# A long convolution's working store kept in runs of four channels instead of runs of two

## The chip, the cores and the metric

The kernel runs on one core of one Trainium2 chip. The metric is the device time of one execution in microseconds (us). The core has a matrix engine (TensorE, PE in the profile, with its weight loads on a row of their own, PEld), a vector engine (DVE), a scalar engine (ACT), a general engine (POOL), and a queue that issues transfers between the chip's memory and the on-chip store (SP). The on-chip store, SBUF, has 128 partitions. TensorE writes its results into PSUM, which has eight banks of 512 floats in each partition. Everything is float32.

TensorE multiplies a *stationary* operand, which is loaded beforehand column by column, by a *moving* operand, which is streamed through. Both are read from SBUF through an access pattern: in each partition, which elements follow one another and with what steps. The change is about these patterns.

## What is computed

```python
def _attn_ref(x, v, pos_emb, w1, w2):              # x, v: (4, 12480, 128); pos_emb: (12480, 64)
    h_mlp = np.maximum(pos_emb @ w1, 0.0) @ w2
    h_filt = h_mlp * np.exp(-0.01 * np.arange(S))[:, None]
    u = x * v
    Uf = np.fft.rfft(u, n=2 * S, axis=1); Hf = np.fft.rfft(h_filt, n=2 * S, axis=0)
    y = np.fft.irfft(Uf * Hf[None], n=2 * S, axis=1)[:, :S, :]
    return x * y

def _moe_ref(x, w_in, w_out):                      # x: (49920, 128); w_in: (128, 2048)
    h = x @ w_in
    return (h * np.cos(h)) @ w_out
```

So: a gated long convolution of each of 128 channels over 12,480 positions, for four batches, and then a feed-forward block over all 49,920 rows.

## The kernel before

**The convolution** is a transform over the product N1 x N2 = 96 x 120, done as four matrix steps per batch, with products by a filter spectrum between the second and the third. All four work in place in one large SBUF tile, `slots`, of 64 channel pairs (`CB`) by 240 places by 2 channels. In the text a step is called by its function:

- `u`: the gated input x*v is folded and written into `slots` by `u_sums` (L406, POOL and DVE), two places with all 64 pairs at a time, from the loaded rows `xt`.
- `f1` (`f1_mm`, L414; evicted by `f1_evict`, L428): for each of 64 channel pairs and each channel i of the pair, the stationary operand is `u[:, b, 0:KE, i]`, which steps over places; the constant table `c1` (192 columns) moves. The result goes back into the same pair's part of `slots`, then called `parts`.
- `f2` (`f2_mm`, L450; `f2_product`, L464): for each of 96 frequencies k the table `w` is stationary and `parts[0:KE, :, k]`, all 64 pairs and both halves r, 256 columns, moves. The result is multiplied by the filter spectrum `h` and written, as `y`, into the places that k has left. The spectrum is computed once, beside the first batch (`f2_both_units`), kept in chip memory (`hd`) and loaded again for the other batches (`f2_units`). Two frequencies, k1 and k1+1, are handled as one unit j.
- `i1` (`i1_mm`, L485; `i1_evict`, L491): for each pair, `slots[0:N2, b, r*N1:..., i]` is stationary and the table `cs` (120 columns) moves; ACT copies one half out of PSUM and DVE writes sum and difference back into `slots`.
- `i2` (`i2_mm`, L510; `i2_out`): for each of 120 output positions in 30 groups of four, two products are accumulated: a made table `t` is stationary and `slots[0:N1, :, place, :]`, 128 columns, moves. The result is multiplied by x and stored.

So `parts` in `f2` and `slots` in `i2` move, and `slots` in `f1` and `i1` is stationary. With the tile laid out as pair, place, channel, a moving read over all channels at one place takes two neighbouring floats (8 bytes), then jumps 1,920 bytes to the next pair. A stationary read over places of one channel steps by two floats.

**The feed-forward block** is a long sequence of 1,568 steps: `moe_up` (a 512-column product into `ph`), three passes of ACT and DVE for the cosine gate, sums on POOL (`moe_sums`) and `moe_down` (products of 128 columns into the banks `acca` and `accb`; seven of them in each pair of steps).

**The order of the work** is written out by hand; every engine takes its instructions in that order. Before about 338 us there is the filter network, the filter's `f1`, the first batch's `f1`, `f2` and `i1`. From then on the steps of the feed-forward block and those of the convolution alternate: after each step `convolve()` (L989) advances the convolution until it has caught up with its share of steps (`F1_STEPS`, `F2_STEPS` and so on, L564). The helper `units` (L535) runs the units of one convolution step: it issues the matmuls of unit j in two parts and, between them, the eviction of unit j-1. From this point on `tiled[0]` is true, and `mm` (L129) issues every matmul as two, one for each half of the output's columns, which work in the array side by side; a float32 matmul is two records in the profile. So a product with 256 moving columns is four records.

Of the kernel before, what the change touches and what calls it, by code (L numbers as in the profile page):

```python
# [9 lines left out]
F32 = mybir.dt.float32  # L10
# [23 lines left out]
def kernel(  # L34
# [63 lines left out]
    CB = D // 2  # L98
    assert R * N2 == S and S + TAPS - 1 <= 2 * M and math.exp(DECAY * TAPS) < 2.0 ** -150
# [13 lines left out]
    hd = dram.tile([N1 // 2, N2, 2, CB, 4], F32, name="hd")  # L113
# [147 lines left out]
    def inverse_tables(pool):  # L261

        t = Tables(pool, nc.gpsimd, 4)
        part = t.whole([P, 1], [[1, 1]], channel_multiplier=1, name="part")
        part4 = t.whole([P, 1], [[1, 1]], base=1, channel_multiplier=4, name="part4")
        step = t.whole([P, P], [[1, P]], name="step")
        mid = t.whole([P, P], [[1, P]], base=-MID, name="mid")
        cs, (rows, tw_t) = third_table(pool), last_tables(pool)
        yield from t.sines(step, part, N2, [(cs[:, 0, 0:H + 1], 1), (cs[:, 1, 0:H + 1], 0)],
                           eighths=slice(0, H + 1, H))  # L270
        yield from t.sines(step[:, 1:H], part, N2,
                           [(cs[:, 0, H + 1:], 0), (cs[:, 1, H + 1:], 1)])
        yield from t.sines(step, part4, 4 * N1,
                           [(rows[:, i, :], q) for i, q in enumerate((0, 1, 2, 3))])
        yield from t.sines(mid, part4, TURN, [(tw_t[:, 0, :], 1), (tw_t[:, 1, :], 0)],
                           eighths=slice(H - 1, N2, H))
        t.finish(len(t.waiting))
        for kept, made in ((csd, cs), (rowsd, rows), (twd, tw_t)):
            nc.sync.dma_start(kept[:, :, :], made[:, :, :])
# [82 lines left out]
    def filter_out(pool, bank, aT, slots, j, w2_sb):  # L362

        ps = bank()
        for i, jj in enumerate((j, H - 1 - j)):
            nc.tensor.matmul(ps[0:FR, i * 2 * D:(i + 1) * 2 * D], aT[:, jj, 0:FR],
                             w2_sb[:, :], start=True, stop=True)
        above = pool.tile([FR, 2, CB, 2], F32, name="above", bufs=2)
        pj = ps[0:FR, :].rearrange("p (n b i) -> p n b i", n=4, i=2)
        nc.scalar.copy(out=above[:, :, :, :], in_=pj[:, 2:4])  # L370
        a = H - 2 - 2 * j
        for place, op in ((a, ALU.add), (ODD + a, ALU.subtract)):
            nc.vector.tensor_tensor(
                slots[0:FR, :, place:place + 2, :].transpose([0, 2, 1, 3]),
                pj[:, 1::-1], above[:, :, :, :], op=op)
# [14 lines left out]
    def clear_gap(u):  # L390

        nc.gpsimd.memset(u[:, :, H:ODD, :], 0.0)
# [13 lines left out]
    def u_sums(u, tiles, a, takers):  # L406
        both = tiles[0][:, :, :].rearrange("p h (n b i) -> p h n b i", n=UA, i=2)
        below, above = both[:, 0, ::-1, :, :], both[:, 1, :, :, :]
        for place, op, e in ((a, ALU.add, takers[0]), (ODD + a, ALU.subtract, takers[1])):
            e.tensor_tensor(u[0:R, :, place:place + UA, :].transpose([0, 2, 1, 3]),  # L410
                            below, above, op=op)


    def f1_mm(ps, u, b, i):  # L414

        mm(ps[0:KE, i * 2 * N1:(i + 1) * 2 * N1], u[:, b, 0:KE, i],
           c1[0:u.shape[0], :, :].rearrange("p r k -> p (r k)"))
# [10 lines left out]
    def f1_evict(ps, b, share):  # L428
        copy, negated = f1_takers(b, share)
        pj = ps[:, 0:4 * N1].rearrange("p (i r k) -> p r k i", i=2, r=2)  # L430
        copy(out=parts[0:ODD, :, :, b, :], in_=pj[0:ODD])
        yield
        copy(out=parts[ODD:KE, 0, :, b, :], in_=pj[ODD:KE, 1])
        negated(parts[ODD:KE, 1, :, b, :], pj[ODD:KE, 0])
        yield

    def f1_evict_filter(ps, b, share):

        copy, negated = f1_takers(b, share)
        pj = ps[:, 0:4 * N1].rearrange("p (i k) -> p k i", i=2)  # L440
        near, far = ftile[:, b, :, :], above[:, b, :, :]
        copy(out=near[0:ODD], in_=pj[0:ODD, 0:N1 + KF])
        copy(out=far[0:ODD], in_=pj[0:ODD, N1 + KF:])
        yield
        copy(out=near[ODD:KE, 0:N1], in_=pj[ODD:KE, N1:])
        negated(near[ODD:KE, N1:], pj[ODD:KE, 0:KF])
        negated(far[ODD:KE], pj[ODD:KE, KF:N1])
        yield

    def f2_mm(ps, w, k1, i, filt=False):  # L450


        k = k1 + i
        pi = ps[0:N2, :].rearrange("p (r b g i) -> p g r b i", r=2, g=2, i=2)[:, i]
        if not filt:
            mm(pi, w[:, i, :], parts[0:KE, :, k])
        elif k < KF:
            both = ftile[0:KE, :, k:k + N1 + 1:N1, :].rearrange("p b r i -> p r b i")
            nc.tensor.matmul(pi, w[:, i, :], both, start=True, stop=True)
        else:  # L460
            for r, src in enumerate((ftile[0:KE, :, k, :], above[0:KE, :, k - KF, :])):
                nc.tensor.matmul(pi[:, r], w[:, i, :], src, start=True, stop=True)

    def f2_product(pool, ps, h, k1, whole):  # L464


        y = parts[0:N2, :, k1:k1 + 2, :, :].rearrange("p r k b i -> p r b (k i)")
        t = pool.tile([N2, 2, CB, 4], F32, name="t", bufs=2)
        uu = ps[0:N2, :].rearrange("p (r b j) -> p r b j", r=2, j=4)
        if whole:  # L470
            for r, (dst, hh) in enumerate(((y, h[:, :, :, :]), (t[:, :, :, :], h[:, ::-1, :, :]))):
                u = uu[:, r]
                twice = bass.AP(tensor=u.tensor, offset=u.offset,
                                ap=[u.ap[0], [0, 2], *u.ap[1:]])
                nc.vector.tensor_tensor(dst, twice, hh, op=ALU.mult)
                yield
        for r, op in ((0, ALU.subtract), (1, ALU.add)):
            if not whole:
                nc.vector.tensor_tensor(y[:, r], uu[:, 0], h[:, r], op=ALU.mult)
                yield  # L480
                nc.vector.tensor_tensor(t[:, r], uu[:, 1], h[:, 1 - r], op=ALU.mult)  # L481
            nc.gpsimd.tensor_tensor(y[:, r], y[:, r], t[:, r], op=op)  # L482
            yield

    def i1_mm(ps, b, i):  # L485
        for r in range(2):
            n = max(N1, CB + CB // 2 + 1) if tiled[0] else N1
            mm(ps[0:n, (i * 2 + r) * N2:(i * 2 + r + 1) * N2],
               slots[0:N2, b, r * N1:r * N1 + n, i], cs[:, r, :])

    def i1_evict(pool, ps, b):  # L491
        pj = ps[0:N1, 0:4 * N2].rearrange("p (i r j) -> p r j i", i=2, r=2)
        other = pool.tile([N1, N2, 2], F32, name="other")
        nc.scalar.copy(out=other[:, :, :], in_=pj[:, 1])
        for h, op in ((0, ALU.add), (1, ALU.subtract)):
            nc.vector.tensor_tensor(slots[0:N1, b, h * N2:(h + 1) * N2, :], pj[:, 0],
# [3 lines left out]
    def i2_mm(ps, t, g, part):  # L500
        for i in range(part * G // 2, (part + 1) * G // 2):
# [8 lines left out]
            for r, place in enumerate(places):  # L510
                mm(ps[0:R, i * D:(i + 1) * D], t[:, i, r, :], slots[0:N1, :, place, :],
# [75 lines left out]
    def f1_units(bank, u, share=0.5, evict=f1_evict):  # L587
# [6 lines left out]
        return units(CB, F1_STEPS, lambda j: None, mm, lambda j, ps: evict(ps, j, share), 2)  # L594

    def f2_units(bank):
        with tc.tile_pool(name="there", bufs=3) as pool:
            ws, hs = {}, {}

            def before(j):  # L600
                ws[j] = pool.tile([KE, 2, N2], F32, name="w")
                nc.sync.dma_start(ws[j][:, :, :], wd[j, :, :, :])
                hs[j] = pool.tile([N2, 2, CB, 4], F32, name="h")
                nc.sync.dma_start(hs[j][:, :, :, :], hd[j, :, :, :, :])

            def mm(j, ps, i):
                if i == 0:
                    ps = bank()
                f2_mm(ps, ws[j], 2 * j, i)
# [3 lines left out]
                             lambda j, ps: f2_product(pool, ps, hs.pop(j), 2 * j, False), 4)  # L613

    def f2_both_units(bank):

        with tc.tile_pool(name="both", bufs=2) as pool:
            ws = {}

            def before(j):  # L620
                ws[j] = pool.tile([KE, 2, N2], F32, name="w")
                for i in range(2):
                    make_w(ws[j][:, i, :], 2 * j + i, half=bank)
                nc.sync.dma_start(wd[j, :, :, :], ws[j][:, :, :])

            def mm(j, ps, i):
                if i == 0:
                    ps = bank(), bank()
                for filt in range(2):
                    f2_mm(ps[filt], ws[j], 2 * j, i, filt=filt == 1)  # L630
                return ps

            def after(j, ps):
                h = pool.tile([N2, 2, CB, 4], F32, name="h", bufs=3)
                nc.scalar.activation(h[:, :, :, :].rearrange("p r b j -> p (r b j)"),
                                     ps[1][0:N2, :], AF.Copy, scale=1.0 / M)
                nc.sync.dma_start(hd[j, :, :, :, :], h[:, :, :, :])
                yield from f2_product(pool, ps[0], h, 2 * j, True)
# [56 lines left out]
    def inverse_units(bank, b):  # L695
# [6 lines left out]
        new = u_units(b + 1, 3, slots[0:R, :, :, :],  # L702
# [10 lines left out]
    def forward_units(bank, back):  # L713
# [3 lines left out]
        yield from f1_units(bank, slots[0:R, :, :, :])  # L717
# [117 lines left out]
    with tc.manual_schedule():  # L835
        with tc.tile_pool(name="psum", bufs=8, space=PSUM) as psum, \
# [5 lines left out]
            slots = spool.tile([P, CB, 2 * N2, 2], F32, name="slots")  # L842
            parts = slots[:, :, 0:2 * N1, :].rearrange("p b (r k) i -> p r k b i", r=2)
            above = slots[:, :, 2 * N1:2 * N2, :]
            aT = above.rearrange("p b j i -> p b (j i)")
# [5 lines left out]
            with tc.tile_pool(name="layers", bufs=1, side="right") as pool:  # L851
# [10 lines left out]
                first_u = u_units(0, 3, slots[0:R, :, :, :],  # L862
# [24 lines left out]
            ftile = fpool.tile([P, CB, N1 + KF, 2], F32, name="ftile")  # L887
            clear_gap(ftile[0:FR, :, :, :])
            with tc.tile_pool(name="out", bufs=1, side="right") as pool:
                for j in range(H // 2):  # L890
                    filter_out(pool, bank, aT, ftile, j, w2_sb)
                    for _ in range(1 + (j % 3 == 0)):
                        next(first_u)
            f1 = f1_units(bank, ftile[0:FR, :, :, :], 0.53, f1_evict_filter)
# [27 lines left out]
            beside(f1_units(bank, slots[0:R, :, :, :], 0.55),  # L922
# [132 lines left out]
```

## Time and profile before

| | us |
|---|---|
| median of 3 runs | 3732.2 (3729.83 to 3733.6) |
| the profiled execution's own time | 3732.51 |
| its span, first to last instruction | 3730.7 |
| PE busy | 3627.8 (97%) |
| DVE busy | 2970.8 (80%) |
| POOL busy | 2787.4 (75%) |
| ACT busy | 2256.0 (60%) |

When the steps of the convolution run (us from the span's start, from the rows' first and last starts):

| batch | f1 | f2 | i1 | i2, with the next batch's u |
|---|---|---|---|---|
| 0 | 114 to 166 | 171 to 269 | 273 to 333 | 338 to 573 |
| 1 | 603 to 766 | 771 to 1098 | 1107 to 1193 | 1194 to 1415 |
| 2 | 1443 to 1593 | 1600 to 1926 | 1935 to 2059 | 2060 to 2281 |
| 3 | 2309 to 2460 | 2467 to 2792 | 2801 to 2943 | 2949 to 3081 |

After 3081 us the feed-forward block runs alone. In the rows `cv` and `ps` are the PSUM banks of the convolution (`cv` once the feed-forward block is running), and the tiles name the step: `cv<-c,slots` is f1, `cv<-slots,w` f2, `cv<-cs,slots` i1, `cv<-slots,tm` i2. The chain of waits is the sequence of instructions that ended last, each followed back to what released it; an engine's time on it is time that the span depends on. A matmul's duration includes the time that it takes to run through the array, which the next one overlaps, so how long a series of them holds TensorE is read from the starts, or from the chain.

### The profile page before, as it was taken

How to read it: one execution, taken by the hardware profiler on the slowest of the kernel's cores; microseconds unless marked ns; L12 is line 12 of the kernel's file. 1: busy time of each engine (PE TensorE's matmuls, PEld its weight loads, DVE VectorE, ACT ScalarE, POOL GpSimd, SP SyncE). 2: the span in 40 equal slices, each digit the busy share in tenths (PEclk: the TensorE clock that was granted, in tenths of full speed). 3: DMA queues.
4: the chain of work that ended last, by engine and by line, in shares of the span. 5: the costliest groups of instructions: out<-in, count | busy, mean ns of one | idle time of the engine just before them, and what ended most of it. 6: DMA issues, size and time to landing. Idle time of an engine off the chain costs nothing.

```text
span 3730.7 us, 101448 instructions
## 1 busy us (share of the span) xinstructions
PE 3627.8 (97%) x40298; PEld 2574.6 (69%) x40298; DVE 2970.8 (80%) x5812; ACT 2256.0 (60%) x4660; POOL 2787.4 (75%) x3271
## 2 busy tenths in 40 slices
PE   7898999999999999999999999999999999999999
PEld 6777776666668776766667776666667786666666
DVE  8887887788887777888887777888887757787777
ACT  5756666665554556665555455665565446666666
POOL 7666987578883887588884788578885447887877
PEclk9999999999999999999999999999999999999999
DMA  6263551012221662022210563012220261000000
GB/s 168 62 182 101 162 157 56 15 53 72 71 62 45 164 172 57 13 63 70 73 55 16 152 171 98 19 38 73 73 64 25 73 175 31 19 19 24 19 24 14
DMA packets 209710, 279.61 MB, mean 75 GB/s; under 512 B 17111, under 2 KB 146535, under 8 KB 209111
## 3 DMA queue, kind: packets, MB, share of 16 engines
q1 hardware_dynamic: 209239, 273.12, 26.0%
q8 instruction: 321, 5.26, 0.6%
q14 instruction: 150, 1.23, 0.1%
HBM read 193.64 MB, written 79.42 MB: 73 GB/s over the span
## 4 chain that ended last, share of the span: by engine, by line
PE 83%; DVE 4%; ACT 1%; POOL 1%; issue 1%; DMA 0%; ACTq 0%; POOLq 0%; DVEq 0%
PE ph L132 30%; PE cv L132 21%; PE accb L787 17%; PE acca L787 13%; PE cv L136 1%; DVE gt L762 1%; DVE gt L756 1%; PE ph L136 1%; ACT gt L755 1%; POOL ts L770 0%; ACT at L744 0%; POOL slots L410 0%; ACT tile L818 0%; DVE t L481 0%; DVE xt L404 0%
## 5 line engine op out<-in xcount | busy, mean ns | idle before, releaser
L755 ACT ACTIVATE gt<-ph 128x512 int32<-128x512 f32 (+1 forms) x1380 | 822.3, 596 | 1138.3 <-PE ph L132 1081.7
L770 POOL TENSOR_TENSOR ts<-gt 128x512 f32<-128x512 f32 (+2 forms) x784 | 1005.2, 1282 | 598.5 <-PE accb L787 526.9
L132 PE MATMUL ph<-at,w_in_sb 128*64 128x512 f32 (+1 forms) x5520 | 1428.2, 592 | 14.2 <-ACT tile L818 6.5
L756 DVE SCALAR_TENSOR_TENSOR gt<-ph,gt 128x512 f32<-128x512 f32 (+1 forms) x1380 | 947.6, 687 | 619.7 <-ACT gt L755 608.6
L761 ACT ACTIVATE gt<-gt 128x512 f32<-128x512 f32 (+1 forms) x1568 | 972.1, 620 | 3.5 <-DVE gt L756 2.9
L762 DVE TENSOR_TENSOR gt<-ph,gt 128x512 f32<-128x512 f32 (+1 forms) x1380 | 934.7, 677 | 0.0
L787 PE MATMUL accb<-ts,w_out_sb 128*64 128x128 f32 (+2 forms) x9408 | 649.7, 272 | 0.0
L774 POOL TENSOR_TENSOR ts<-gt,ts 128x256 f32<-128x256 f32 (+2 forms) x784 | 573.8, 732 | 61.5
L773 POOL TENSOR_TENSOR ts<-ts,gt 128x256 f32<-128x256 f32 (+2 forms) x784 | 573.6, 732 | 61.5
L787 PEld LDWEIGHTS acca<-gt,w_out_sb 128*64 128x64 f32 x6272 | 399.3, 137 | 267.1 <-issue 232.2
L787 PEld LDWEIGHTS accb<-ts,w_out_sb 128*64 128x64 f32 x9408 | 543.5, 137 | 0.0
L787 PE MATMUL acca<-gt,w_out_sb 128*64 128x128 f32 (+2 forms) x6272 | 479.2, 272 | 0.0
L787 PEld LDWEIGHTS accb<-gt,w_out_sb 128*64 128x64 f32 x3136 | 225.8, 137 | 253.0 <-issue 199.7
L132 PEld LDWEIGHTS ph<-at,w_in_sb 128*64 128x64 f32 x5520 | 354.0, 137 | 34.6 <-ACT tile L818 14.7
L482 POOL TENSOR_TENSOR slots<-slots,t 120x256 f32<-120x256 f32 x384 | 281.1, 738 | 120.3 <-DVE t L481 72.4
L132 PEld LDWEIGHTS cv<-slots,tm 96*64 96x64 f32 (+1 forms) x3840 | 245.5, 128 | 127.0 <-issue 114.7
L787 PE MATMUL accb<-gt,w_out_sb 128*64 128x128 f32 (+1 forms) x3136 | 311.1, 273 | 4.3 <-DVE ot L808 2.8
L787 PE MATMUL acca<-ts,w_out_sb 128*64 128x128 f32 (+1 forms) x3136 | 308.5, 272 | 1.7 <-POOL ts L773 1.6
L132 PE MATMUL cv<-slots,tm 96*64 96x128 f32 (+1 forms) x3840 | 278.3, 287 | 8.8 <-POOL tm L306 5.6
L132 PEld LDWEIGHTS cv<-cs,slots 120*64 120x64 f32 (+1 forms) x3072 | 167.9, 125 | 61.0 <-issue 59.0
L787 PEld LDWEIGHTS acca<-ts,w_out_sb 128*64 128x64 f32 x3136 | 201.6, 137 | 3.1 <-POOL ts L773 2.9
L132 PEld LDWEIGHTS cv<-c,slots 104*60 104x60 f32 (+1 forms) x1536 | 110.4, 137 | 124.6 <-issue 95.6
(145 smaller groups left out, 4113.5 us busy)
## 6 DMA issues: line engine op xcount, KB each, us to landing
h<-hd SPq DMA_DIRECT2D x144, 240.0 KB
tm<-td SPq DMA_DIRECT2D x96, 312.0 KB
xt<-in_x_dram SPq DMA_DIRECT2D x120, 208.0 KB
vt<-in_v_dram SPq DMA_DIRECT2D x120, 208.0 KB
xs<-in_x_dram SPq DMA_DIRECT2D x120, 208.0 KB
zd<-xs SPq DMA_DIRECT2D x119, 208.0 KB
tile<-zd SPq DMA_DIRECT2D x96, 256.0 KB
w<-wd SPq DMA_DIRECT2D x144, 116.2 KB
```

The costliest lines, as they stand in the source:

```text
L132: nc.tensor.matmul(dst[lo:hi], left[:, lo:hi], right, start=start, stop=stop)
L136: nc.tensor.transpose(dst, src, ident[0:n, 0:n])
L482: nc.gpsimd.tensor_tensor(y[:, r], y[:, r], t[:, r], op=op)
L755: nc.scalar.activation(turns, ph[:, 0:m], AF.Identity, bias=phase)
L756: nc.vector.scalar_tensor_tensor(out=part, in0=ph[:, 0:m], scalar=phase, in1=turns, op0=ALU.add, op1=ALU.subtract)
L761: nc.scalar.activation(part, part, AF.Sin, scale=scale)
L762: nc.vector.tensor_tensor(part, ph, part, op=ALU.mult)
L770: nc.gpsimd.tensor_tensor(ts[:, 0:2, 0:half], gt[:, :, half:2 * half], gt[:, 0, 0:2 * half].rearrange("p (h n) -> p h n", h=2), op=ALU.sub ...
L773: nc.gpsimd.tensor_tensor(t[2], t[1], b11, op=ALU.add)
L774: nc.gpsimd.tensor_tensor(t[3], b21, t[2], op=ALU.subtract)
L787: nc.tensor.matmul(acc[h * CB:(h + 1) * CB, place, 0:r], w_out_sb[:, pair, weight, :], right[:, h * r:(h + 1) * r], start=(pair == 0 and i ...
```

## The change

The tile keeps its size, but its order is now: channel quad (32), half (2), place within the half (120), pair within the quad (2), channel within the pair (2). All four channels of a quad stand together at a place: 16 bytes, and 3,840 bytes from quad to quad. In particular:

- `u`, from the second batch on, and the results of `f1` and `i1` are written into this order, so that what moves in `f2` and `i2` is read in runs of four floats instead of two. `f1`'s stationary operand from the second batch on then steps by four floats (16 bytes) instead of two.
- `y`, the product in `f2`, is written differently: `made_y` gives each pair of the quad 96 frequencies by two channels in one piece, so that `i1`'s stationary operand still steps by two floats.
- The first batch's `u` and the filter stay in the old order (`apart`, `apart_f`) until `f1` has read them.
- Since `y` of unit j now covers the places j and 48+j, the units take their frequencies in another order: 0 and 1, 48 and 49, 2 and 3, 50 and 51, and so on (`f2_first`). The row tables of the inverse are permuted to match, by five small instructions on POOL and two on DVE while the tables are made.
- Where a step's result covers what the quad's other pair has yet to read (`f1` from the old order, and `i1`), the eviction of the even pair is issued one part later, after the odd pair's matmuls.
- `h` and `t` are laid out as quad, real or imaginary half, pair, four; the transfers keep their number and size.

TensorE's instructions and SP's transfers stay the same in number; in the first batch, where the filter's product is in one matmul for half of the frequencies and in two for the others, these now alternate.

```diff
-    hd = dram.tile([N1 // 2, N2, 2, CB, 4], F32, name="hd")
+    hd = dram.tile([N1 // 2, N2, Q, 2, 2, 4], F32, name="hd")
...
-        part4 = t.whole([P, 1], [[1, 1]], base=1, channel_multiplier=4, name="part4")
+        part4 = t.whole([P, 1], [[1, 1]], base=1, channel_multiplier=2, name="part4")
+        order = pool.tile([P, 3], U32, name="order")
+        nc.gpsimd.iota(order[:, 0:1], pattern=[[1, 1]], base=0, channel_multiplier=1)
+        terms = pool.tile([P, 2], F32, name="terms")
+        for bit, factor in ((1, 2.0), (2, N1 - 2.0)):
+            nc.vector.tensor_scalar(out=order[:, bit:bit + 1], in0=order[:, 0:1], scalar1=bit,
+                                    scalar2=3, op0=ALU.bitwise_and, op1=ALU.bitwise_and)
+            nc.gpsimd.tensor_scalar(out=terms[:, bit - 1:bit], in0=order[:, bit:bit + 1],
+                                    scalar1=factor, scalar2=0.0, op0=ALU.mult, op1=ALU.add)
+            nc.gpsimd.tensor_tensor(part4[:, :], part4[:, :], terms[:, bit - 1:bit], op=ALU.add)
...
     def u_sums(u, tiles, a, takers):
-        both = tiles[0][:, :, :].rearrange("p h (n b i) -> p h n b i", n=UA, i=2)
+        run = 2 if len(u.shape) == 4 else 4
+        both = tiles[0][:, :, :].rearrange("p h (n c j) -> p h n c j", n=UA, j=run)
...
-            e.tensor_tensor(u[0:R, :, place:place + UA, :].transpose([0, 2, 1, 3]),
-                            below, above, op=op)
+            there = u[0:R, :, place:place + UA]
+            there = there.rearrange("p c n e i -> p n c (e i)") if run == 4 else \
+                there.transpose([0, 2, 1, 3])
+            e.tensor_tensor(there, below, above, op=op)
...
     def f1_mm(ps, u, b, i):
-        mm(ps[0:KE, i * 2 * N1:(i + 1) * 2 * N1], u[:, b, 0:KE, i],
+        ub = u[:, b] if len(u.shape) == 4 else u[:, b // 2, :, b % 2]
+        mm(ps[0:KE, i * 2 * N1:(i + 1) * 2 * N1], ub[:, 0:KE, i],
            c1[0:u.shape[0], :, :].rearrange("p r k -> p (r k)"))
...
-    def f1_evict(ps, b, share):
+    def f1_evict(ps, b, share, late):
+        if late:
+            yield
         copy, negated = f1_takers(b, share)
         pj = ps[:, 0:4 * N1].rearrange("p (i r k) -> p r k i", i=2, r=2)
-        copy(out=parts[0:ODD, :, :, b, :], in_=pj[0:ODD])
+        copy(out=parts[0:ODD, :, :, b // 2, b % 2, :], in_=pj[0:ODD])
...
     def f2_mm(ps, w, k1, i, filt=False):
-        pi = ps[0:N2, :].rearrange("p (r b g i) -> p g r b i", r=2, g=2, i=2)[:, i]
+        pi = ps[0:N2, :].rearrange("p (r c e g i) -> p g r c e i", r=2, e=2, g=2, i=2)[:, i]
         if not filt:
             mm(pi, w[:, i, :], parts[0:KE, :, k])
...
-    def f2_product(pool, ps, h, k1, whole):
-        y = parts[0:N2, :, k1:k1 + 2, :, :].rearrange("p r k b i -> p r b (k i)")
-        t = pool.tile([N2, 2, CB, 4], F32, name="t", bufs=2)
-        uu = ps[0:N2, :].rearrange("p (r b j) -> p r b j", r=2, j=4)
+    def f2_first(j):
+        return j + (N1 // 2 - 1) * (j % 2)
+
+    def f2_product(pool, ps, h, j, whole):
+        y = made_y[0:N2, j]
+        t = pool.tile([N2, Q, 2, 2, 4], F32, name="t", bufs=2)
+        uu = ps[0:N2, :].rearrange("p (r c e q) -> p r c e q", r=2, e=2, q=4)
...
     def i1_mm(ps, b, i):
         for r in range(2):
             n = max(N1, CB + CB // 2 + 1) if tiled[0] else N1
+            start = 4 * N2 * r + 2 * N1 * (b % 2) + i
             mm(ps[0:n, (i * 2 + r) * N2:(i * 2 + r + 1) * N2],
-               slots[0:N2, b, r * N1:r * N1 + n, i], cs[:, r, :])
+               flat[0:N2, b // 2, start:start + 2 * n:2], cs[:, r, :])

     def i1_evict(pool, ps, b):
+        if b % 2 == 0:
+            yield
...
-            nc.vector.tensor_tensor(slots[0:N1, b, h * N2:(h + 1) * N2, :], pj[:, 0],
+            nc.vector.tensor_tensor(slots[0:N1, b // 2, h * N2:(h + 1) * N2, b % 2, :], pj[:, 0],
                                     other[:, :, :], op=op)
...
-                mm(ps[0:R, i * D:(i + 1) * D], t[:, i, r, :], slots[0:N1, :, place, :],
+                mm(ps[0:R, i * D:(i + 1) * D], t[:, i, r, :], slots[0:N1, :, place].rearrange("p c e i -> p c (e i)"),
                    start=(r == 0), stop=(r == 1))
...
-            slots = spool.tile([P, CB, 2 * N2, 2], F32, name="slots")
-            parts = slots[:, :, 0:2 * N1, :].rearrange("p b (r k) i -> p r k b i", r=2)
-            above = slots[:, :, 2 * N1:2 * N2, :]
-            aT = above.rearrange("p b j i -> p b (j i)")
+            halves = spool.tile([P, Q, 2, N2, 2, 2], F32, name="slots")
+            slots = halves.rearrange("p c h n e i -> p c (h n) e i")
+            parts = halves[:, :, :, 0:N1].rearrange("p c r k e i -> p r k c e i")
+            above = halves[:, :, :, N1:N2]
+            flat = halves.rearrange("p c h n e i -> p c (h n e i)")
+            made_y = halves[:, :, :, 0:N1].rearrange("p c r n e i -> p c r (n e i)").rearrange(
+                "p c r (e t q) -> p t c r e q", e=2, q=4)
+            apart = flat.rearrange("p c (e n i) -> p (c e) n i", e=2, i=2)
+            aT = apart[:, :, 2 * N1:2 * N2, :].rearrange("p b j i -> p b (j i)")
```

## The prediction

> **What bounds the kernel now.** I read the page first: which engine is busy, and whose work the chain of waits consists of.
>
> ```profile
> PE 3627.8 (97%) x40298; PEld 2574.6 (69%) x40298; DVE 2970.8 (80%) x5812; ACT 2256.0 (60%) x4660; POOL 2787.4 (75%) x3271
> ...
> PE 83%; DVE 4%; ACT 1%; POOL 1%; issue 1%; DMA 0%; ACTq 0%; POOLq 0%; DVEq 0%
> ```
>
> TensorE holds the chain for 83% of the span, so what the change does to a matmul counts, and what it does to the other engines counts only where they are on the chain. I then read the chain in order of time in the four steps, because there a series of matmuls shows how long it holds TensorE (start, us, what). First the second batch's i2, then f2, then f1, then i1:
>
> ```profile
> 2104.02 0.88 PE accb L787 x16
> 2104.90 0.86 PE ph L132 x4
> 2105.76 1.00 PE cv L132 x16
> ```
>
> ```profile
> 1700.36 0.51 PE cv L132 x4
> 1700.87 0.66 PE acca L787 x12
> 1701.53 0.86 PE ph L132 x4
> ...
> 1704.12 0.48 PE cv L132 x4
> ...
> 1706.11 0.48 PE cv L132 x4
> ```
>
> ```profile
> 1454.68 0.65 PE cv L132 x8
> 1455.33 0.88 PE accb L787 x16
> 1456.20 0.86 PE ph L132 x4
> ```
>
> ```profile
> 1108.62 0.82 PE cv L132 x16
> ...
> 1111.17 1.23 PE cv L132 x24
> ```
>
> The yardstick is the feed-forward block, which moves contiguous data: 4 records of 512 columns take 0.86 us and 16 of 128 take 0.88, so 2,048 columns cost 0.86 to 0.88. f1 (8 x 192 columns, contiguous table moving) should take 0.65 and does; i1 (24 x 120) should take 1.23 and does. But i2 moves the same 2,048 columns as `accb` in runs of two floats and takes 1.00, 0.12 more; f2 moves 1,024 columns in runs of two and takes 0.48 to 0.51 where half of 0.86 is 0.43. So the two steps whose moving operand is in short runs, and only these, lose 11 to 19%. The durations by shape agree:
>
> ```profile
> L787 PE MATMUL accb<-ts,w_out_sb 128*64 128x128 f32 x9216 | 638.8, 272 | 0.0
> ...
> L132 PE MATMUL cv<-slots,tm 96*40 96x128 f32 x1920 | 274.9, 287 | 0.0
> ...
> L132 PE MATMUL cv<-slots,w 124*56 124x256 f32 x576 | 187.4, 407 | 0.0
> ...
> L132 PEld LDWEIGHTS cv<-c,slots 104*64 104x64 f32 x768 | 103.0, 138 | 112.9 <-issue 85.6 <-PE cv L132 9.7 <-ACT at L744 3.8
> ...
> L132 PEld LDWEIGHTS cv<-cs,slots 120*33 120x33 f32 x1536 | 157.9, 111 | 38.3 <-issue 38.3
> ...
> L787 PEld LDWEIGHTS accb<-ts,w_out_sb 128*64 128x64 f32 x9408 | 543.5, 137 | 0.0
> ```
>
> i2 has 287 ns against 272 for 128 columns. f2 has 407, where the line from 272 (128 columns) to 593 (512) gives 379. The last three rows are weight loads, for later: with a step of two floats 64 columns take 138 ns, contiguous 137.
>
> **The change part by part.** The sum is made against the profiled execution, 3732.5 us (span 3730.7), 0.3 us from the median of 3732.2.
>
> *i2's moving reads, runs of two become runs of four.* Two records work side by side, so a unit of 16 records gains at most 8 x 15 ns = 0.12 us by the rows, and 1.00 - 0.875 = 0.125 by that piece of the chain; other pieces are 0.96 for 14 and 0.98 for 15, so I take 0.11. There are 240 units (two column halves of 1,920 records, by 16). In batches 1 to 3 these are on the chain: between 1194 and 1415 us its share by line is 26.9% for `cv` L132, 59.4 us for 60 units, which is all of them (60 x 0.98 = 58.8). So 180 x 0.11 = 19.8 us. In batch 0 (338 to 573) the share is 17.8%, 41.8 us, seven tenths: 60 x 0.11 x 0.7 = 4.6.
>
> *f2's moving reads.* By the rows 2 x 28 = 56 ns for four records, by the chain 50 to 80; I take 55. 288 sets (1,152 records / 4) give 15.8 us. The chain holds 12.9, 12.0 and 13.0% of the three stretches for `cv`, 42.6, 39.2 and 42.3 us, of about 96 x 0.49 = 47: 88%. There DVE's `gt` rows hold 4 to 7%, and they will hold more once TensorE is shorter. So 13.9 us. In the first batch f2 is not in halves: a matmul there streams alone, half as fast, and TensorE waits for `w` from DVE (13.1 us of PEld's waits there); I take nothing.
>
> Does a run of four cost what contiguous data cost? [...] Gain bounds: 0, if the jump to another quad costs as much as two jumps now, and all of 45 us (28.8 + 16.3 by the rows at full realisation). [...]
>
> *f1's stationary reads, step of two floats becomes four.* 1,536 load records, two side by side, 768 pairs. No row shows a step of four. Loads of 33 and 64 columns take 111 and 138 ns, 0.87 ns a column and 82 fixed. In f1 the pairs follow at 0.65/4 = 163 ns. In the block they follow at 0.88/8 = 110 ns with loads of 137, and hold nothing up: a load may outlast the spacing by 27. So f1's load is free up to 190 ns, 1.69 ns a column, twice the present. Lower bound 0. [...] I take 1. Dearer than that is a rival below.
>
> *New waits.* In f2 DVE's product of unit j-1 waits at odd j for the first matmul of j, issued just before it (72 times); in i1 the even pair's eviction waits for the odd pair's second matmul (96 times in the loop). Behind it in DVE's queue stands the block's next `gt` pass, for which ACT and then the sums on POOL wait. But on DVE these instructions come after two `gt` passes (0.69 + 0.68 us) that themselves wait for ACT's 0.60 after `ph`, about 2 us after `ph` ends, and by then TensorE has done its 0.5 (f2) or 1.0 us (i1). Only at one step in 16 does the convolution stand ahead of `moe_up`: (72 + 96)/16 = 10 waits of at most 1 us. A PSUM bank of an even pair is held half a unit longer, with three banks in turn; where `moe_turn` takes one, about three times in each i1, TensorE may wait up to 1 us: 9 us at most. Together 0 to 19; I take 2, since L496 on DVE and L494 on ACT now wait little in all (19.0 and 26.5 us).
>
> *Writes and reads of DVE, ACT and POOL.* Counts and elements stay. DVE writes runs of two at 16-byte steps in i1 and f1: the nearest row, L373, writes runs of two far apart, 256 elements in 411 ns, and L481 contiguous ones in 413: nothing. ACT's write of eight-float runs (L359, 480 elements, 571) against contiguous (L352, 557) bounds its f1 evictions at +14 ns x 35 to 96, 1 us, covered (ACT busy 107 of 167 us in f1). POOL's `y` sum and `u_sums` lie between 734 (contiguous, L773) and 759 (runs of two, L410): within 25 ns x 480 = 12 us of POOL time either way, and POOL holds 1% of the chain: 0, or 0.1 of it. The seven table instructions, at most 5 x 0.55 + 2 x 0.28 = 3.3 us (from L209's and L151's rows), lie in a stretch where POOL is busy 34 of 52 us: 0. Before the loop the late evictions fall where TensorE is far ahead, 42 matmuls on end in i1, with eight banks: 0, at most 2. Transfers stay in number and size. If all these covers were gone, 1 + 12 + 3 + 2 = 18 us would come on top.
>
> Sum: -19.8 - 4.6 - 13.9 + 1 + 2 = -35. 3732.5 - 35 = 3697; the median is the same within 0.3.
>
> [...]
>
> **The rivals.**
>
> *The gain is half.* A jump between quads costs something too, or DVE and POOL take over in f2. For it: the excess in f2 varies, 0.48 or 0.51, so it depends on more than the run; and POOL is busy 288 of 330 us there. Against: contiguous rows show none. 3732.5 - 19 + 3: about 3716.
>
> *Two floats a piece are enough already, and something else slows i2 and f2.* They also share a moving operand that jumps between channels while DVE and POOL write the same tile. For it: before the loop f2 shows 407 ns too, and the filter's product (L459) 388, although only one matmul streams there and the starts show no loss. [...] Against: f1 and i1 read the same tile as stationary without loss. Then 3732.5 - 0 + 3: 3735, between 3730 and 3740.
>
> *Slower: f1's loads become the bound.* If a column that lies alone in its piece takes x ns, a pair is held for 64x + 82 - 190 ns beyond 1.69 ns, 768 times. At 2.4 ns a column (2.8 times the present) the loss is 46 ns x 768 = 35 us and cancels the gain; that is the point from which it decides. At 3.5 it is 116 x 768 = 89 us: 3732.5 - 38 + 2 + 89 = 3785. At 2.7 the time is 3732.5 - 38 + 2 + 50 = 3746. For it: nothing in the trace shows a step of four, and the block's loads run close to their spacing. [...]
>
> **How the numbers follow.** Forecast (3687 to 3706) 0.60; half 0.18; no cause 0.10; slower 0.12. The range starts at 3686 (all of 45 us) and reaches to 3736, through the third case's middle, leaving the slower case and some tails, under 0.2, out. The likeliest case's own range is 3687 to 3706. 0.2% is 7.5 us, about what a measurement of this kernel can tell: faster is the first two, 0.78; same 0.10; slower 0.12.
>
> **What would show it.** Right: in the chain, i2's 16 records at 0.88 and f2's four at 0.43 to 0.44; by shape, 272 and about 379 ns; f1's eight still 0.65, with loads of at most 193 ns. TensorE's busy time falls by some 40 us, the stretches of i2 by about 6.5 us each in batches 1 to 3. Wrong: f1's eight above 0.68 (the slower rival), i2 still at 1.00 (not the runs), `cv` waiting for `slots` L496 in i1 (the held bank), or DVE and POOL filling what TensorE gives up in f2.

## The result, and the profile after

The changed kernel takes 3737.0 us in the median (3734.81 to 3740.22, 22 runs), the kernel before 3731.9 us (3729.48 to 3736.14, 22 runs). The ratio is 1.0014, with a 95% interval of 1.0007 to 1.0020. So the change makes the kernel 5 us slower, clear of the noise but within the 0.2% that the prediction calls "same", where 3697 us, 35 us less, was forecast. The profiled execution after took 3735.07 us, its span is 3732.9 us (3730.7 before).

The page's busy times and its shares of the chain, of the kernel after:

```profile
PE 3603.4 (97%) x40298; PEld 2567.4 (69%) x40298; DVE 2995.6 (80%) x5814; ACT 2274.8 (61%) x4660; POOL 2781.6 (75%) x3276
...
PE 80%; DVE 6%; ACT 2%; issue 1%; POOL 1%; DMA 0%; ACTq 0%; POOLq 0%; DVEq 0%; SPq 0%
```

TensorE is busy 24.4 us less, and yet the span is not shorter. On the chain TensorE went from 83 to 80%, DVE from 4 to 6 and ACT from 1 to 2: something else than matmuls now ends the waits.

The chain in order of time shows that the reads became as fast as forecast. First i2 of the second batch, then f2, then f1 (start, us, what):

```profile
2103.43 0.88 PE cv L133 x16
2104.31 0.87 PE accb L817 x16
```

```profile
1702.32 0.86 PE ph L133 x4
1703.17 0.43 PE cv L133 x4
```

```profile
1454.64 0.65 PE cv L133 x8
1455.30 0.66 PE acca L817 x12
```

i2's 16 records take 0.88 us, where they took 1.00; contiguous `accb` takes 0.87 beside them. f2's four take 0.43 and no longer 0.48 to 0.51. f1's eight take 0.65, as before. The groups by shape (busy us, mean ns | idle just before, and what ended it):

```profile
L133 PE MATMUL cv<-slots,tm 96*40 96x128 f32 x1920 | 251.1, 275 | 0.0
...
L133 PE MATMUL cv<-cs,slots 120*64 120x120 f32 x1536 | 185.0, 267 | 25.3 <-DVE slots L524 24.4
...
L133 PE MATMUL cv<-slots,w 124*56 124x256 f32 x576 | 172.8, 381 | 0.0
...
L133 PEld LDWEIGHTS cv<-c,slots 104*64 104x64 f32 x768 | 136.2, 195 | 90.0 <-issue 64.6 <-PE cv L133 8.5 <-ACT gt L791 5.3
```

i2 has 275 ns (287 before), f2 381 (407). f1's loads went from 138 to 195 ns. The row that gives the answer is the second, i1's: TensorE is idle 25.3 us ahead of these matmuls, 24.4 of it ended by L524, DVE's sums in `i1_evict`. Before, the same row had 0.4:

```profile
L132 PE MATMUL cv<-cs,slots 120*64 120x120 f32 x1536 | 177.9, 266 | 0.4 <-DVE slots L496 0.4
```

Where the time lies, by the steps' first starts as in the table of before (a step ends where the next one starts; sums over the batches, which add up to the two spans):

| stretch, us | before | after | difference |
|---|---|---|---|
| up to i2 of batch 0 | 338.3 | 338.6 | +0.3 |
| i2, four | 894.6 | 872.6 | -22.0 |
| f1, three | 482.8 | 487.3 | +4.5 |
| f2, three | 1004.0 | 991.6 | -12.4 |
| i1, three | 361.3 | 393.0 | +31.7 |
| the feed-forward block alone | 649.7 | 649.8 | +0.1 |

So 34 us were gained in i2 and f2, and 37 lost, 32 of them in i1.

What happens in i1 is seen in its second stretch. First the chain there, in order of time, then the timeline of the same place (start, us, engine, line, what, xcount [idle before <- what ended it]):

```profile
1966.83 0.88 PE ph L133 x4
...
1967.80 0.61 ACT gt L785
1968.40 0.02 issue
1968.42 0.69 DVE gt L786
1969.12 0.60 DVE gt L792
1969.71 0.32 DVE slots L524
1970.04 0.14 issue
1970.17 0.61 PE cv L133 x8
```

```profile
1967.52 0.99 PE L133 MATMUL cv<-cs,slots 120*64 120x120 f32 x16
...
1968.42 0.69 DVE L786 SCALAR_TENSOR_TENSOR gt<-ph,gt 128x512 f32<-128x512 f32 x1 [1.26 <-ACT gt L785]
1969.03 0.68 DVE L792 TENSOR_TENSOR gt<-ph,gt 128x512 f32<-128x512 f32 x1
1969.63 1.02 DVE L524 TENSOR_TENSOR slots<-cv,other 96x240 f32<-96x240 f32 x3
1970.17 0.61 PE L133 MATMUL cv<-cs,slots 120*64 120x120 f32 x8 [1.66 <-DVE slots L524]
```

This is a step of the feed-forward block in which the convolution issues three parts, the two of one pair (x16) and the first of the next (x8). The x8 waits 1.66 us for a sum that ends at about 1970. That sum is held by nothing of its own: DVE was idle for 1.26 us before L786, and then had to do the two gate passes, which wait for ACT's pass, which waits for `ph`. The sum stands behind them in DVE's queue.

The order explains which steps are hit. Pair b, even, has its second sum issued one part later than before, just ahead of the first part of pair b+2. Pair b+3 takes the bank of pair b, since the convolution has three banks in turn. I1_STEPS is 0.8, so parts come in steps of 2, 3, 2, 3, ten units in eight steps. Where a step of three parts begins with pair b+2, its third part wants pair b's bank in the very step whose gate passes stand ahead of pair b's sum on DVE. That is so once in ten units. In the trace the waits stand there: units 5 and 15 in the first i1, 7, 17, 27, 37 and 47 in the second, 3, 13, ... 63 in the third, 14 in all, with 1.86 to 1.94 us from one matmul's start to the next. 14 x 1.8 = 25 us, beyond the usual spacing of 0.1. Smaller ones make up the rest: 11 of 0.64 to 0.74 us after `ph`, where 0.41 is usual, and 25 of 0.22, all of them at odd units from unit 25 of the first i1 and unit 53 of the second on, where the units follow one another without the block's work between them.

### The profile page after: what moved, and what is told of

Read it like the earlier page. It is cut to its first block, busy times and chain, and to the rows that moved or that the text cites. A ratio compares the mean times of both kernels' runs of the same rounds, so it can differ in the third digit from the quotient of the medians.

```text
span 3732.9 us, 101727 instructions
## 1 busy us (share of the span) xinstructions
PE 3603.4 (97%) x40298; PEld 2567.4 (69%) x40298; DVE 2995.6 (80%) x5814; ACT 2274.8 (61%) x4660; POOL 2781.6 (75%) x3276
## 3 DMA queue, kind: packets, MB, share of 16 engines
q1 hardware_dynamic: 209239, 273.12, 25.8%
## 4 chain that ended last, share of the span: by engine, by line
PE 80%; DVE 6%; ACT 2%; issue 1%; POOL 1%; DMA 0%; ACTq 0%; POOLq 0%; DVEq 0%; SPq 0%
PE ph L133 29%; PE cv L133 20%; PE accb L817 17%; PE acca L817 12%; DVE gt L792 2%; DVE gt L786 2%; PE cv L137 1%; ACT gt L785 1%; PE ph L137 1%; DVE slots L524 0%; DVE xt L414 0%; DVE t L506 0%; ACT at L774 0%; POOL ts L800 0%; POOL slots L424 0%
## 5 line engine op out<-in xcount | busy, mean ns | idle before, releaser
L786 DVE SCALAR_TENSOR_TENSOR gt<-ph,gt 128x512 f32<-128x512 f32 (+1 forms) x1380 | 947.6, 687 | 578.7 <-ACT gt L785 566.8
L133 PEld LDWEIGHTS cv<-slots,tm 96*40 96x40 f32 (+1 forms) x3840 | 228.5, 128 | 126.6 <-issue 113.1
L133 PE MATMUL cv<-slots,tm 96*40 96x128 f32 (+1 forms) x3840 | 254.9, 276 | 9.3 <-POOL tm L316 6.0
L133 PEld LDWEIGHTS cv<-c,slots 104*64 104x64 f32 (+1 forms) x1536 | 140.7, 191 | 107.9 <-issue 82.2
L133 PE MATMUL cv<-cs,slots 120*64 120x120 f32 (+1 forms) x3072 | 186.4, 267 | 25.3 <-DVE slots L524 24.4
```

The source lines that it names most:

```text
L133: nc.tensor.matmul(dst[lo:hi], left[:, lo:hi], right, start=start, stop=stop)
L786: nc.vector.scalar_tensor_tensor(out=part, in0=ph[:, 0:m], scalar=phase, in1=turns, op0=ALU.add, op1=ALU.subtract)
```

## The experiments

Theories for the lost time: **A**, the held bank (the even pair's eviction is late, and the bank comes free behind the gate passes); **B**, the new wait for data (the sums wait for the odd pair's matmul, and hold DVE's queue); **C**, the forms of access themselves (f1's loads with a step of four, ACT's and DVE's writes at 16-byte steps).

**e1: the even pair's two sums together.** The changed kernel, but both sums are issued in one part, so that the second is no longer half a unit late beyond the first. The wait for the odd pair's matmul, B, stays.

```diff
         for h, op in ((0, ALU.add), (1, ALU.subtract)):
             nc.vector.tensor_tensor(slots[0:N1, b // 2, h * N2:(h + 1) * N2, b % 2, :], pj[:, 0],
                                     other[:, :, :], op=op)
-            yield
+            if h == 1 or b % 2 == 1:
+                yield
```

> One edit to the changed kernel: in i1 the two sums of an even pair are issued together, right after the odd pair's second matmul, instead of the second one a part later. Theory A (a PSUM bank held too long: TensorE needs the even pair's bank three units later, and the second sum stands behind the next step's gt passes in DVE's queue): the waits of TensorE for L524, 24 us, go and with the stalls the 32 us that i1 grew by; 3737 - 25 to 32 = 3705 to 3712. Theory B (the new wait of the sums for the odd pair's matmul is what costs): it is still there, 3737, or more. Theory C (f1's loads of 195 ns, ACT's slower writes and DVE's slower products use the gain up): 3737.

Measured: 3714.0 us (3712.67 to 3715.64), against 3731.0 for the kernel before on the same chip (so in each experiment: what stands behind "against" is the kernel before, run beside it); ratio 0.9953 (0.9938 to 0.9968). i1 takes 368 us instead of 393, all else is as in the changed kernel within 4 us. Its row:

```profile
L133 PE MATMUL cv<-cs,slots 120*64 120x120 f32 x1536 | 182.5, 267 | 1.2 <-DVE slots L524 0.8
```

One `yield` is worth 23 us, and the idle time that DVE ended went from 24.4 to 0.8 us. All waits of 1.9 us are gone. A holds, B can't be the main cause, as the wait is still there. What is left of i1's loss, 6 us, is in the smaller waits: five of 0.65 us after `ph` (0.41 is the usual spacing there), 26 of 0.22 and eight of 0.3 to 0.5 (0.1 is usual for both); that is 5 x 0.23 + 26 x 0.12 + 8 x 0.28 = 6.5.

**e2: the late eviction alone.** The kernel before, with nothing of the change but the delay. No layout, and no new data wait: here the delay is needless.

```diff
     def i1_evict(pool, ps, b):
+        if b % 2 == 0:
+            yield
         pj = ps[0:N1, 0:4 * N2].rearrange("p (i r j) -> p r j i", i=2, r=2)
```

> One edit to the kernel before, layout untouched: i1's eviction of even pairs is issued one part later. There is no new wait on data in it, only a bank held half a unit longer. Theory A: i1 grows by about 32 us in all, 3732 + 32 = 3764. Theories B and C: 3732, within 5.

Measured: 3758.8 us (3757.27 to 3760.88) against 3731.0; ratio 1.0074 (1.0057 to 1.0090). i1 takes 389 us, +28, and everything else stands as before. The row has the same idle time, and the 14 long waits stand at the same units:

```profile
L132 PE MATMUL cv<-cs,slots 120*64 120x120 f32 x1536 | 181.1, 267 | 25.2 <-DVE slots L498 24.4
```

The delay alone costs 28 us, without any of the change's data waits or layouts. That is most of what the changed kernel lost in i1, so A is shown from both sides: put in alone it costs 28, taken out it gives 23. The 25 small waits of 0.22 us are not in this run; they are taken up under e4.

**e3: y in steps of four too.** The change's layout, but y stays in place in the order of its frequencies, so i1's stationary operand steps by four floats; no pair covers the other's data, and no i1 eviction is late.

```diff
-        y = made_y[0:N2, j]
+        y = halves[0:N2, :, :, 2 * j:2 * j + 2].rearrange("p c r n e i -> p c r (n e i)").rearrange(
+            "p c r (e q) -> p c r e q", e=2)
...
-               flat[0:N2, b // 2, start:start + 2 * n:2], cs[:, r, :])
+               halves[0:N2, b // 2, r, 0:n, b % 2, i], cs[:, r, :])
...
     def i1_evict(pool, ps, b):
-        if b % 2 == 0:
-            yield
```

> The changed kernel without its special form of y: y stays in runs of four in the places of its own frequencies, frequencies in their old order, no permuted tables, no late eviction in i1; i1's stationary operand then steps by four floats. f1's loads with this step took 188 to 195 ns. i1's pairs follow every 103 ns and can bear loads of about 103 + 28 = 131: 64 ns too much for 1,536 pairs is 98 us, so 3705 + 98 = 3803. If loads overlap further, as they do not hold f1 up, nothing is lost in i1 and the gain of the moving reads stays: 3700.

Measured: 3753.9 us (3752.31 to 3755.69) against 3731.0; ratio 1.0060 (1.0045 to 1.0075). Neither number came: the stationary step of four costs much less than the one and much more than nothing. i2 and f2 gain as in the changed kernel (874 and 992 us), i1 loses 22 us in the loop with no wait of TensorE for DVE, and the stretch before the loop is 30 us longer. The rows of i1, in the loop and before it (`ps`):

```profile
L133 PE MATMUL cv<-cs,slots 120*64 120x120 f32 x1536 | 200.4, 281 | 0.0
...
L133 PEld LDWEIGHTS cv<-cs,slots 120*64 120x64 f32 x1536 | 199.2, 210 | 12.1 <-issue 6.4 <-ACT ot L820 1.3
...
L133 PEld LDWEIGHTS ps<-cs,slots 120*96 120x96 f32 x512 | 91.0, 273 | 3.5 <-POOL slots L499 3.5
```

In the loop the loads take 210 ns instead of 138, but the matmuls' busy time grows only from 177.9 to 200.4 us, 15 ns a pair: the rest of the load lies beside other work. Before the loop 96 columns take 273 ns instead of 171, and there the matmuls' row grows from 56.0 to 91.3 us. So the change's own form of y, which makes the late eviction necessary, avoids a cost of 52 us (30 before the loop, 22 in it); it is the price that it pays for this, 32 us, that the other runs bring down.

**e4: the copy early, the sums together.** As e1, but ACT's copy out of PSUM is issued where it stood before, and only the sums are late.

```diff
     def i1_evict(pool, ps, b):
-        if b % 2 == 0:
-            yield
...
         nc.scalar.copy(out=other[:, :, :], in_=pj[:, 1])
+        if b % 2 == 0:
+            yield
         for h, op in ((0, ALU.add), (1, ALU.subtract)):
...
-            yield
+            if h == 1 or b % 2 == 1:
+                yield
```

> As the first of these, and ACT's copy of the even pair out of PSUM is issued where it stood before the change, one part ahead of the sums. Theory A: as the first, 3705 to 3712, or up to 4 us less, since the sums then never wait for the copy. Theory B and C: 3737.

Measured: 3712.9 us (3710.14 to 3716.55) against 3731.0; ratio 0.9950 (0.9935 to 0.9965); i1 takes 368 us. This is the fastest kernel of the study, though not apart from e1. It says something on B, in the row of DVE's sums:

```profile
L524 DVE TENSOR_TENSOR slots<-cv,other 96x240 f32<-96x240 f32 x384 | 132.0, 396 | 25.8 <-PE cv L133 25.8
```

DVE does wait for the odd pair's matmul, 25.8 us in all, and TensorE's idle time is still 1.2 us. So the new wait is real and nearly free, but not quite. The 26 spacings of 0.22 us are here too, as in e1 and in the changed kernel (25). The kernel before and e2, which have no such data wait, show one to three of them, and e5, which has it but frees the bank without DVE, shows one. In e1 the trace has the order of events: the even pair's sums start as the odd pair's matmuls come to their end, and the matmul that takes the even pair's bank starts 0.15 us after the second sum ends. Where no gate pass stands between, the wait for data is thus itself a held bank, of 26 x 0.12 = 3 us. The row doesn't show it as idle time, since a record of 267 ns reaches over a spacing of 0.22; it shows it as busy time, 182.5 us for 177.9. With the 28 us of the late eviction, these 3 are nearly all of the 32 that i1 lost.

**e5: the sums late, the bank free.** As in the changed kernel the even pair's sums are issued late, one by one, but ACT copies both halves out of PSUM at once, one part ahead of the sums, so that the bank doesn't wait for DVE.

```diff
     def i1_evict(pool, ps, b):
+        pj = ps[0:N1, 0:4 * N2].rearrange("p (i r j) -> p r j i", i=2, r=2)
         if b % 2 == 0:
+            held = pool.tile([N1, 2, N2, 2], F32, name="held")
+            nc.scalar.copy(out=held[:, :, :, :], in_=pj)
             yield
+            near, other = held[:, 0], held[:, 1]
...
-            nc.vector.tensor_tensor(slots[0:N1, b // 2, h * N2:(h + 1) * N2, b % 2, :], pj[:, 0],
+            nc.vector.tensor_tensor(slots[0:N1, b // 2, h * N2:(h + 1) * N2, b % 2, :], near,
                                     other[:, :, :], op=op)
```

> The changed kernel, with the sums of i1 where it has them, the second one a part late. But ACT copies both halves of an even pair out of PSUM at once, so the bank comes free without DVE, and DVE sums from the copies. Theory A in its narrow form (it is the bank that TensorE waits for): the 1.9 us stalls and the waits for DVE's sums in i1 go although the sums stand where they stood; 3737 - 23 to 32 = 3705 to 3714. If instead TensorE or DVE is held by the order of DVE's queue or by the sums' new wait for the odd pair's matmul, the stalls stay: 3737. ACT's longer copy (480 elements, some 0.55 us for 0.35) is 96 x 0.2 = 19 us of an engine that is idle 40% of the time.

Measured: 3718.3 us (3717.44 to 3722.68) against 3732.6; ratio 0.9962 (0.9949 to 0.9975). i1 takes 367 us, as in e1, though the sums come as late as in the changed kernel. So it is the bank and not the lateness of the result that TensorE waits for. Two costs are its own: the stretch before the loop is about 9 us longer, and DVE's sums are slower where both operands lie in SBUF:

```profile
L133 PE MATMUL cv<-cs,slots 120*64 120x120 f32 x1536 | 179.9, 266 | 8.6 <-DVE slots L529 8.6
...
L529 DVE TENSOR_TENSOR slots<-held 96x240 f32<-96x240 f32 x256 | 141.5, 582 | 23.8 <-ACT held L521 14.4 <-PE cv L133 5.1 <-PE ps L133 4.2
...
L529 DVE TENSOR_TENSOR slots<-cv,other 96x240 f32<-96x240 f32 x192 | 70.1, 394 | 0.0
```

The 8.6 us of waiting that are left stand mostly ahead of even units, at every tenth one (0.5 to 1.0 us from start to start, once 1.9). By the rotation that is an odd pair's bank, which DVE still frees, now behind the slower sums; this last was not tested.

**e6: the control for e1.** The kernel before, with the even pair's two sums issued in one part, but not late; the edit is e1's.

> A control on the kernel before, layout and times of issue otherwise untouched: the two sums of an even pair issued together, not late. If issuing them together is worth something in itself, 3731 - 5 or less; by theory A there is nothing to free here, so 3731 within 4.

Measured: 3732.5 us (3729.53 to 3736.1) against 3732.6; ratio 1.0000 (0.9991 to 1.0010). Issuing the sums together is no gain by itself; in e1 it is one because it undoes the late release.

**e7: f1's stationary step alone.** The kernel before, with f1's operand in the loop read in steps of four floats.

```diff
-        mm(ps[0:KE, i * 2 * N1:(i + 1) * 2 * N1], u[:, b, 0:KE, i],
+        left = u[:, b, 0:KE, i]
+        if tiled[0]:
+            two = u[:, b - b % 2:b - b % 2 + 2].rearrange("p b n i -> p (b n i)")
+            start = i + 464 * (b % 2)
+            left = two[:, start:start + 4 * KE - 3:4]
+        mm(ps[0:KE, i * 2 * N1:(i + 1) * 2 * N1], left,
```

> The kernel before with one thing of the change: in batches 1 to 3 f1's stationary operand is read with a step of four floats instead of two. It takes elements of the two neighbouring pairs, not the right ones, so the output is not the reference's; the number of columns, matmuls, waits and evictions is the same. If the loads explain the 5 us by which f1's stretches grew in the changed kernel: loads of 188 to 195 ns, f1's eight matmuls still 0.65 us, 3732 + 3 to 5. If those 5 us come from the slower writes of ACT and DVE in f1's evictions (460 to 552 and 540 to 575 ns): 3732 within 1.

Measured: 3735.8 us (3733.85 to 3737.26, 11 runs) against 3732.6 (15 runs); ratio 1.0008 (0.9999 to 1.0017), so the whole run can't tell it from nothing. The stretches say more: f1 takes 486.2 us in all, against 482.8 before and 487.3 after, and most of the difference, 2.7 us, lies in the first one. All profiles divide in this way: the six with the step of four have 486.2 to 487.3 us, the three without it 482.8 to 483.9. The load's row is the changed kernel's:

```profile
L132 PEld LDWEIGHTS cv<-c,slots 104*64 104x64 f32 x768 | 136.2, 195 | 88.7 <-issue 67.1 <-PE cv L132 8.3 <-POOL slots L410 4.6
```

In the chain eight matmuls still take 0.65 us. So the step is worth some 3 of the 4.5 us; how the remaining 1 us splits between the slower writes of ACT and DVE and chance was not settled.

A fourth bank for the convolution, the plainest way to free A, was not tried: the eight banks that the kernel opens are in use, as `acca`, `accb`, three `ph` and three `cv`.

## Why the prediction was wrong

The forecast of 3697 us missed by 40; the time lies just outside its range of 3686 to 3736, and in the bound of "same", which had 0.10. By the steps of the sum:

| term | forecast | measured |
|---|---|---|
| i2's moving reads | -19.8 - 4.6 | -22.0 |
| f2's moving reads | -13.9 | -12.4 |
| f1's stationary reads, and the writes there | +1 | +4.5 |
| new waits (the bank among them) | +2 (0 to 19) | +31.7 |
| before the loop | 0 to +2 | +0.3 |
| sum | -35 | +2 |

**i2 and f2: right, in the cause and nearly in size.** No row of before moves runs of four; that they would cost what contiguous data cost was the author's estimate. The runs showed it: 0.88 us for i2's 16 records, where `accb` takes 0.87, and 0.43 for f2's four, half of the 0.86 of `ph`; by the rows 275 ns, where `accb` has 273, and 381, where the line between 128 and 512 columns gave 379. The distance between the quads shows as no more than these 2 ns. The stretches are 34 us shorter, where 38.3 were forecast. The gain was 4 us in the first batch's i2, for which 4.6 was taken, and 6 in each of the others, where 6.6 was. Where a single matmul streams, no gain shows: the first batch's f2, whose reads did change, has 407 ns before and after, and its matmuls start 0.22 us apart in both, as those of L366 do, which move as many contiguous columns at 379 ns.

**The data waits: right where the block stands between.** DVE waits for the odd pair's matmul, 14.0 us in `i1_evict` and 0.9 in `f2_product`, and e4 shows 25.8 us of such waiting with TensorE idle for 1.2. There the argument held: these instructions stand behind the gate passes, and by then TensorE is done. It left out the stretches of i1 in which units follow one another without the block: there the wait held the bank and cost 3 us (e4).

**The held bank: the step that failed.** The prediction had the mechanism in the sentence "A PSUM bank of an even pair is held half a unit longer, with three banks in turn; where `moe_turn` takes one, about three times in each i1, TensorE may wait up to 1 us: 9 us at most", and named `cv` waiting for the sums in i1 as its sign. Both factors of the bound were wrong, and the value then taken, 2, left it out almost wholly. The count: it wasn't the block's turn that made the bank scarce, but the step of three parts that begins with the unit after next, once in ten units, 14 times and not nine, besides the small ones. The price: the wait isn't the half unit by which the sum was moved, but the time until DVE has done the two gate passes that now stand ahead of it, which start only after `ph` and ACT, 1.9 us and not 1. The same gate passes were what made the data wait harmless: here what covered a wait for data on DVE delayed the release of a bank. The reason given for taking 2, that the sums waited little before (19.0 and 26.5 us), spoke of DVE's and ACT's waits and not of who waits for them.

**f1: small, above the forecast.** No row of before has a step of four. The +1 in the sum and the 193 ns among the signs were the author's estimates, and no run shows them. The runs showed loads of 195 ns, eight matmuls still at 0.65 us, and stretches that grew by 4.5 us; e7 puts 3 of it on the step, by its stretches, while the interval of its whole time touches none. ACT's write, taken at +14 ns at most, went from 460 to 552 and from 326 to 378 ns: the rows chosen to bound it had runs of eight floats, these have runs of two at 16-byte steps. It is covered, as said.

**The rivals.** "Two floats are enough", a run of two as good as one of four, gave 3735 and so the right time for a wrong reason: the reads did gain (287 to 275 and 407 to 381 ns). The slower case rested on f1's loads, with each column alone among four floats, and they weren't the loss: eight matmuls stayed at 0.65 us. The case that happened, gain in full and a wait in i1 that eats it, was not among the rivals at all; it stood as a bound of 19 inside a sum, and in none of the chances.

## What to carry to other kernels

Here an eviction that was moved later in DVE's in-order queue held its PSUM bank until the gate passes that then stood ahead of it were done (0.69 and 0.68 us, behind ACT's 0.60), and the matmul that wanted the bank started 1.86 to 1.94 us after the one before it. So walk the issue order for a whole period of the steps, find the unit that wants the bank next, and price the wait by the queue ahead, not by the distance moved. Where a result has to be late, let its last reads of the bank be issued together and ahead of the next block of work (e1: 3714.0 us, where the changed kernel takes 3737.0), or let another engine empty the bank (e5: 3718.3): here one `yield` made 0.6% of the whole. And a bound several times larger than the value taken is a rival and deserves a chance.

## What the runs showed of the hardware

- Moving runs of 8 bytes (before) gave records 4 to 7% longer than runs of 16 bytes (after) where two column halves work side by side (i2: 287 against 275 ns, f2: 407 against 381). By the chain's starts the loss was 12 to 19% (1.00 against 0.88 us for 16 records, and 0.48 to 0.51 against 0.43 for four). Where one matmul streams alone, in the first batch's f2, the row is 407 ns with either.
- A stationary step of 16 bytes instead of 8 lengthened a load by 41% for 64 columns in f1 (138 to 195 ns, after and e7), by 52% in i1 (138 to 210, e3) and by 60% for 96 columns (171 to 273 ns, e3). In f1, where the pairs follow each other at 163 ns (0.65 us / 4), eight matmuls still took 0.65 us, and the stretches grew by some 3 us in all (e7). In i1 in the loop, where they follow at 103 ns (1.23 us / 12 pairs), it cost 15 ns a pair (e3), and of the 102 ns more for 96 columns 69 came through in i1 before the loop, where 512 matmuls stream alone (56.0 to 91.3 us, e3).
- ACT took 552 ns to write 384 elements in runs of two floats at 16-byte steps (after), where it took 460 before; DVE, in the same eviction, 575, where it took 540.
- DVE's sum of 240 elements took 582 ns with both operands in SBUF and 394 with one of them in PSUM (e5, L529).
